# Splitting one granule's load over the DMA engines unevenly in a two-layer decode kernel

## The chip, the cores and the metric
The kernel runs on one core of a Trainium2 chip. The metric is the device time of one execution in microseconds. Sixteen DMA engines bring data from HBM to SBUF; the core's five compute engines are TensorE (PE), VectorE (DVE), ScalarE (ACT), GpSimd (POOL) and SyncE (SP), of which SP here only issues transfers.

## The reference
One decode step of two layers, each an attention block and a dense block, with the same weights and the same caches in both layers:

```python
B, Sq, D = 8, 1, 512
Hq, Hkv, Sk, Dh = 32, 8, 8192, 128
...
q = ((x @ wq).reshape(B, Sq, Hq, Dh)).transpose(0, 2, 1, 3)
scores = einsum("bhqd,bhkd->bhqk", q, repeat(k_cache, 4, axis=1)) * Dh ** -0.5
o = einsum("bhqk,bhkd->bhqd", softmax(scores), repeat(v_cache, 4, axis=1))
attention = o.transpose(0, 2, 1, 3).reshape(B, Sq, Hq * Dh) @ wo
dense = einsum("bsf,fd->bsd", silu(einsum("bsd,df->bsf", x, w1)), w2)
...
x = x + attention(layernorm(x));  x = x + dense(layernorm(x))     # twice
```

All inputs are bfloat16. K and V together hold 2 x 8 x 8 x 8192 x 128 elements, 268 MB, and every key and value is needed in both layers.

## The kernel before
**Granules and slots.** The 8192 keys of one head and batch are cut into four granules of 2048 keys. A granule of K or V is 512 KB: 128 partitions, on each 16 consecutive keys of 128 elements, which is one contiguous row of 4096 bytes in HBM and in SBUF. The SBUF tensor `ARENA` has 28 slots of this size. Some loads bring two neighbouring granules at once into two slots (`d.n == 2`, rows of 8192 bytes).

**Order.** A task is (layer, batch, head). `make_tasks` orders the 128 tasks so that the two layers of each batch interleave: heads 3 to 7 of a batch are kept heads, which are done for layer 0, then, once the batch's query for layer 1 is known, for layer 1. Of the kept heads' K granules (20, heads 3 to 7) the transposed keys stay in their slots from layer 0 to layer 1; of V only the last three granules stay (head 7, granules 1 to 3). One K granule (head 7, granule 3) is parked in PSUM in between. Thus K of head 7, granule 0 is read from HBM once for each batch, and V of it twice. The order of all loads comes from a planner (`lay_loads`), which gives each one a slot, a place in the order and a time from which the slot is free.

**Work on a granule.** Keys are transposed on PE (line 551) and copied back over the granule by ACT (line 560) and DVE (line 562); scores are matmuls on line 585; the softmax runs over the whole head (lines 596 to 634); the product with V is on line 645. The order of the keys inside a granule does not matter as long as K and V have the same. The dense blocks and projections run between the tasks (lines 760 and 732).

**Loads.** All big loads are issued on SP's queue by `issue` through the helper `dma` (line 407). `dma` waits (line 88, in `Sync.wait`) for what last used the slot, takes a token of the slot's own semaphore, which counts 16 for each transfer, and issues the transfer. A consumer waits until the semaphore has reached the token's value. `issue_until` issues loads in the planned order, and its place among the compute steps sets which readers a load waits for.

The program itself is a long unrolled list of instructions, which the chip fetches by DMA while it runs: these transfers appear in the profile as queues of the kind "instruction".

## Time and profile before

| What | Value |
|---|---|
| Median of 3 runs | 1132.41 us (1131.87 to 1133.05) |
| Profiled execution: time / span | 1138.0 us / 1136.2 us |
| PE, DVE, ACT busy | 82%, 49%, 43% of the span |
| Granted TensorE clock, mean | 0.933 |
| Read from HBM | 452.47 MB, 398 GB/s over the span |
| Loads of one granule (V / K) | 206 / 184, 512 KB each |
| Loads of two granules (V / K) | 141 / 84, 1024 KB each |

The profile is of one execution. A busy share says how long an engine had something to do, not that it was the limit. The queue lines give DMA packets (one for each contiguous row, and one of 4 bytes for each engine's addition to a semaphore), their bytes and the time that they took as a share of all 16 engines' span. A packet's record has its start, its length, its size and its queue, but not its engine.

### The profile page before, as it was taken

What the parts mean: (1) busy time and instruction counts of PE and PEld (TensorE: products, weight loads), DVE (VectorE), ACT (ScalarE), POOL (GpSimd) and SP (SyncE); (2) the same over time, 40 slices, a digit from 0 to 9 for tenths busy, and PEclk for the clock granted to TensorE, in tenths of its full rate; (3) what the DMA queues carried; (4) which work ended last, traced back from release to release, by engine and by line L of the source; (5) the groups of instructions that cost most, each with busy time, mean ns of one, the idle gap of its engine ahead of it and who ended that gap; (6) DMA issues with size and microseconds to landing.
All of it is one profiled execution on the core that took longest, in us unless ns stands there. A gap on an engine that the chain in (4) does not pass through costs nothing.

```text
span 1136.2 us, 42713 instructions
## 1 busy us (share of the span) xinstructions
PE 930.5 (82%) x18792; PEld 699.6 (62%) x18792; DVE 555.3 (49%) x1710; ACT 492.2 (43%) x778; POOL 117.8 (10%) x300
## 2 busy tenths in 40 slices
PE   6687888888888788888888888888888887878886
PEld 4366656666576556666566655666566665766565
DVE  6444554456344544446444554445444463445544
ACT  5354424554255424554245433554245442544332
POOL 0000110011100110001100111001100111001100
PEclk9699988999899988999699998999899997999987
DMA  9999999999999999999999999999999999999995
GB/s 377 416 414 414 393 406 419 417 396 404 416 418 412 334 400 419 417 409 383 399 419 412 387 399 420 418 412 397 407 418 414 398 401 413 418 413 376 400 418 221
DMA packets 91805, 455.25 MB, mean 401 GB/s; under 512 B 10204, under 2 KB 10468, under 8 KB 62308
## 3 DMA queue, kind: packets, MB, share of 16 engines
q1 hardware_dynamic: 91604, 452.51, 98.9%
q8 instruction: 148, 2.42, 0.9%
q14 instruction: 37, 0.30, 0.1%
q10 hardware_dynamic: 16, 0.01, 0.0%
HBM read 452.47 MB, written 0.01 MB: 398 GB/s over the span
## 4 chain that ended last, share of the span: by engine, by line
DMA 49%; PE 33%; DVE 8%; ACT 4%; issue 4%; SPq 2%; POOL 0%; POOLq 0%; ACTq 0%; DVEq 0%
DMA arena<-in_A_v_cache_dram 29%; DMA arena<-in_A_k_cache_dram 18%; PE TPp L551 15%; PE SCp L585 8%; DVE arena L562 7%; PE OTp L645 4%; ACT arena L560 3%; PE MISC L760 3%; DMA wq<-in_A_wq_dram 2%; PE TPp L625 2%; SPq L407 2%; ACT P L609 1%; PE KEPTp L551 1%; DVE small L634 0%; PE MISC L732 0%
## 5 line engine op out<-in xcount | busy, mean ns | idle before, releaser
L560 ACT COPY arena<-TPp 128x1024 bf16<-128x1024 bf16 x344 | 348.3, 1013 | 388.8 <-PE TPp L551 385.6
L562 DVE COPY arena<-TPp 128x1024 bf16<-128x1024 bf16 x344 | 238.0, 692 | 335.7 <-PE TPp L551 333.7
L551 PE MATMUL TPp<-ident,arena 128*128 128x128 bf16 x5504 | 378.8, 223 | 25.9 <-DMA arena<-in_A_k_cache_dram 19.5
L551 PEld LDWEIGHTS TPp<-ident,arena 128*128 128x128 bf16 x5504 | 318.4, 100 | 112.5 <-issue 64.2
L645 PE MATMUL OTp<-PT,arena 128*128 128x32 bf16 x8192 | 291.3, 179 | 59.4 <-DMA arena<-in_A_v_cache_dram 54.1
L645 PEld LDWEIGHTS OTp<-PT,arena 128*128 128x128 bf16 x8192 | 251.9, 97 | 133.7 <-DMA arena<-in_A_v_cache_dram 100.7
L585 PE MATMUL SCp<-arena,QB 128*32 128x512 bf16 x2048 | 221.5, 421 | 73.0 <-DVE arena L562 27.2
L609 ACT ACTIVATE P<-SCp,small 128x512 bf16<-128x512 f32 x128 | 88.0, 688 | 205.6 <-DVE small L607 169.3
L596 DVE TENSOR_REDUCE small<-SCp 128x1 f32<-128x512 f32 x128 | 88.4, 691 | 96.2 <-PE SCp L585 95.0
L585 PEld LDWEIGHTS SCp<-arena,QB 128*32 128x32 bf16 x2048 | 60.3, 95 | 115.5 <-ACT arena L560 52.1
L600 POOL PARTITION_ALL_REDUCE small<-small x128 | 47.7, 373 | 576.9 <-DVE small L598 576.9
L617 POOL PARTITION_ALL_REDUCE small<-small x128 | 55.4, 433 | 327.4 <-DVE at L659 147.9
L625 PE MATMUL TPp<-ident,P 128*128 128x128 bf16 x512 | 55.0, 235 | 30.4 <-ACT arena L560 17.4
L625 PEld LDWEIGHTS TPp<-ident,P 128*128 128x128 bf16 x512 | 31.4, 103 | 40.1 <-ACT arena L560 24.1
L629 DVE COPY PT<-TPp 128x256 bf16<-128x256 bf16 x128 | 37.3, 291 | 21.6 <-PE TPp L625 19.9
L615 DVE TENSOR_SCALAR small<-small 128x4 f32<-128x4 f32 x128 | 28.7, 224 | 31.1 <-ACT P L609 30.8
L598 DVE TENSOR_SCALAR small<-small 128x4 f32<-128x4 f32 x128 | 29.4, 230 | 4.5
L773 DVE STREAM_TRANSPOSE MISC<-MISC 128x128 f32<-128x128 f32 (+2 forms) x40 | 22.0, 550 | 18.0 <-PE MISC L760 18.0
L605 DVE TENSOR_TENSOR small<-small 128x4 f32<-128x4 f32 x128 | 20.0, 156 | 20.9 <-POOL small L600 20.9
L609 ACT ACTIVATION_READ_ACCUMULATOR P<-SCp,small 128x1 f32 x128 | 24.7, 193 | 0.0
L760 PE MATMUL MISC<-wo,at 128*32 128x128 bf16 x1024 | 24.6, 221 | 0.0
L560 ACT COPY arena<-KEPTp 128x1024 bf16<-128x1024 bf16 x16 | 16.2, 1012 | 14.3 <-PE KEPTp L551 10.9
(102 smaller groups left out, 331.6 us busy)
## 6 DMA issues: line engine op xcount, KB each, us to landing
arena<-in_A_v_cache_dram SPq DMA_DIRECT2D x141, 1024.0 KB, 19.6
arena<-in_A_v_cache_dram SPq DMA_DIRECT2D x206, 512.0 KB, 7.0
arena<-in_A_k_cache_dram SPq DMA_DIRECT2D x184, 512.0 KB, 9.4
arena<-in_A_k_cache_dram SPq DMA_DIRECT2D x84, 1024.0 KB, 22.0
arena<-in_A_wo_dram SPq DMA_DIRECT2D x8, 512.0 KB, 12.7
wq<-in_A_wq_dram SPq DMA_DIRECT2D x1, 4096.0 KB, 25.3
w<-in_B_w_dram SPq DMA_DIRECT2D x1, 1792.0 KB, 23.3
arena<-in_B_w_dram SPq DMA_DIRECT2D x3, 512.0 KB, 17.3
```

What stands on the lines that cost most here:

```text
L551: lambda c=c: pe.transpose(tpv[:, c, :], chunk(slot, h * GRP + c), ident[:, :])
L560: op(act, lambda: act.copy(dst, bank[:, :]), reads=[rt], writes=[r_half(slot, h)])
L562: op(dve, lambda: dve.tensor_copy(dst, bank[:, :]), reads=[rt], writes=[r_half(slot, h)])
L585: lambda t=t: pe.matmul(SCp[bank][t * QR:(t + 1) * QR, :], QB[qn][:, NGRAN - 1 - k:NGRAN - 1 - k + QR], keys[:, t * KB:(t + 1) * KB], star ...
L596: op(dve, lambda: dve.tensor_reduce(mxp[st][:, :], SCp[bank][:, :], AX.X, ALU.max), reads=[f"SC{bank}"], writes=[f"mxp{st}"])
L600: op(pool, lambda: pool.partition_all_reduce(mxa[st][:, :], mxr[st][:, :], 128, bass.bass_isa.ReduceOp.max), reads=[f"mxr{st}"], writes=[f ...
L609: op(act, lambda: act.activation(P[:, :], SCp[bank][:, :], ACT.Exp, bias=nb[st][:, 0:1], scale=SM_SCALE, accum_out=rs[st][:, :]), reads=[f ...
L617: op(pool, lambda: pool.partition_all_reduce(ssa[st][:, :], ssm[st][:, :], 128, bass.bass_isa.ReduceOp.add), reads=[f"ssm{st}"], writes=[f ...
L625: lambda c=c: pe.transpose(tpv[:, c, :], P[:, c * 128:(c + 1) * 128], ident[:, :])
L629: op(dve, lambda: dve.tensor_copy(PT[:, :, :, :], tpv.rearrange("p c (t q) -> p c t q", q=QR)[:, :, :, 0:NGRAN * REP]), reads=[f"TP{tb}"], ...
L645: lambda n=n, cc=cc: pe.matmul(otp, chunk(slot, n), PT[:, cc % CPB, (cc // CPB) % NT, cc // (CPB * NT)::NGRAN].unsqueeze(2).to_broadcast([ ...
L760: lambda t=t, col=col, w=w, start=start, stop=stop: pe.matmul(MISC[t * QR:(t + 1) * QR, 0:math.prod(w.shape[1:])], spread(col), w, start=s ...
```

## The change
The load of granule 0 of head 7, of K and of V, becomes two transfers into the same slot. The first fills partitions 0 to 47 with the granule's rows 0 to 47 in another order: partition 8a + p gets row 6p + a, and the source's access pattern has the six values of a as its outermost dimension. The second fills partitions 48 to 127 with rows 48 to 127 as usual. Both add to the slot's semaphore, and consumers wait for both. All other loads stay one transfer; `dma` takes a list of parts for this.

```diff
+FEW = 6
+SHARE = 8
+UNEVEN = (7, 0)
...
-    def dma(eng, out_ap, in_ap, counter, reads=(), writes=()):
+    def dma(eng, parts, counter, reads=(), writes=()):
...
         syn.acquire(eng, reads, writes)
-        tok = counter.next_tok()
-        eng.dma_start(out_ap, in_ap).then_inc(counter.sem, 16)
+        for out_ap, in_ap in parts:
+            tok = counter.next_tok()
+            eng.dma_start(out_ap, in_ap).then_inc(counter.sem, 16)
         syn.release(tok, reads, writes)
         return tok
...
         dst = ARENA[:, d.slot * SLOT:(d.slot + d.n) * SLOT]
-        dma(sp, dst, src, slsem[d.slot],
+        parts = [(dst, src)]
+        if (d.g, d.k) == UNEVEN:
+            assert d.n == 1
+            m = FEW * SHARE
+            parts = [(dst[0:m], src[0:m].rearrange("(p a) e -> a p e", a=FEW)), (dst[m:128], src[m:128])]
+        dma(sp, parts, slsem[d.slot],
             writes=[r_half(s, h) for s in range(d.slot, d.slot + d.n) for h in range(HALVES)])
```

The other calls of `dma` only put their one pair into a list.

More of the change, by code (lines that the diff above doesn't have):

```diff
@@ L441, in _ @@
         def _(sync_eng):
-            dma(act, Xr[0:B, :], x_in, wsem["x"], writes=["P"])
+            dma(act, [(Xr[0:B, :], x_in)], wsem["x"], writes=["P"])
             op(pool, lambda: pool.memset(ident[:, :], 0.0), writes=["ident"])
@@ L480, in load_wq @@
             def load_wq():
-                dma(sp, wq_sb[:, :, :], A_wq.rearrange("(kt p) n -> p kt n", p=128), wsem["wq"], writes=["wq"])
+                dma(sp, [(wq_sb[:, :, :], A_wq.rearrange("(kt p) n -> p kt n", p=128))], wsem["wq"], writes=["wq"])
             def load_rest():
-                dma(sp, w1_sb[:, :, :], B_w1.rearrange("(kt p) f -> p kt f", p=128), wsem["w1"], writes=["w1"])
-                dma(sp, w2_sb[:, FT - FT % RUN:, :], B_w2[(FT - FT % RUN) * 128:, :].rearrange("(ft p) d -> p ft d", p=128),
+                dma(sp, [(w1_sb[:, :, :], B_w1.rearrange("(kt p) f -> p kt f", p=128))], wsem["w1"], writes=["w1"])
+                dma(sp, [(w2_sb[:, FT - FT % RUN:, :], B_w2[(FT - FT % RUN) * 128:, :].rearrange("(ft p) d -> p ft d", p=128))],
                     wsem["w2"], writes=["w2"])
@@ L492, in load_runs @@
                 for (w, _to, _name, g), s in zip(runs, lent):
-                    dma(sp, ARENA[:, s * SLOT:(s + 1) * SLOT],
-                        w[g * RUN * 128:(g + 1) * RUN * 128, :].rearrange("(p i) d -> p (i d)", i=RUN), slsem[s],
+                    dma(sp, [(ARENA[:, s * SLOT:(s + 1) * SLOT],
+                              w[g * RUN * 128:(g + 1) * RUN * 128, :].rearrange("(p i) d -> p (i d)", i=RUN))], slsem[s],
                         writes=[r_half(s, h) for h in range(HALVES)])
```

## The prediction
> **What bounds the kernel now.** I read the busy table by slices first, then the DMA queues, the chain that ended last, the DMA issues, and the waits of SP's queue.

> ```profile
> DMA  9999999999999999999999999999999999999995
> GB/s 377 416 414 414 393 406 419 417 396 404 416 418 412 334 400 419 417 409 383 399 419 412 387 399 420 418 412 397 407 418 414 398 401 413 418 413 376 400 418 221
> DMA packets 91805, 455.25 MB, mean 401 GB/s; under 512 B 10204, under 2 KB 10468, under 8 KB 62308
> ## 3 DMA queue, kind: packets, MB, share of 16 engines
> q1 hardware_dynamic: 91604, 452.51, 98.9%
> q8 instruction: 148, 2.42, 0.9%
> q14 instruction: 37, 0.30, 0.1%
> ...
> DMA 49%; PE 33%; DVE 8%; ACT 4%; issue 4%; SPq 2%; POOL 0%; POOLq 0%; ACTq 0%; DVEq 0%
> ```

> The DMA row is full in 39 of 40 slices, and the transfers hold the largest part of the chain. The one line that matters for this change is q8: 148 packets that are no data but instruction fetches. 37,584 of the 42,713 instructions are PE's matmuls and weight loads, so nearly all of q8 is PE's program.

> ```profile
> SPq L88 <- PE OTp L645: 426.1, 232, 6.8
> SPq L88 <- PE SCp L585: 138.2, 142, 6.9
> ```

> ```profile
> L407 SPq DMA_DIRECT2D arena<-in_A_v_cache_dram x347: 327/328/4997, 14.8 to 1102.8; - x174
> ```

> The queue that issues the loads waits over 560 us for PE to release slots (first two lines, from the waits of SP's queue: total, times, longest), and an issue itself takes 0.33 us (the line from the view of source line 407: shortest, median, longest in ns). So SP has time to spare; slots and the 16 DMA engines set the pace.

> A share of 0.9% hides that fetches need not be spread evenly, so I went through the trace's packets one by one. A 4096-byte row of a granule takes 159 ns and the next row of the same engine starts 3 or 4 ns before its end: 155.5 ns a row. By this and by the count of eight rows and one mark (4 bytes, for the semaphore) per engine and granule, each engine's packets can be followed from the start to about 120 us. Three things come out.
> - A q8 fetch (16,384 bytes, mean 1.05 us) sits on one engine and sets that engine back by 1.54 to 1.61 us, in 11 clear cases of the first 120 us: ten rows, far more than its bytes. The others lose nothing.
> - The first eight fetches fell on eight different engines; the ninth and tenth on the two that had the first two (they were equally late, so their order can't be told). So I read a rotation over eight of 16. The small q14 fetches (8,192 bytes; 0.68 to 0.98 us lost) fell on others, as far as it can be told.
> - The spread from first to last of the 16 landings of one granule averages 2.9 us and reaches 5.3 us, with some six engines close together in front. It grows over the stretches of each batch where the queue is ten deep, and is drained where it is four deep.

> So the eight fetch engines are the bound: 148 / 8 = 18.5 fetches x 1.56 us = 28.9 us over the run in which the rest must wait, 3.6 us in each batch's cycle of about 140 us. That agrees with the spread.

> **The change, part by part.** K of granule (7,0) is read once a batch (kept for layer 1), V twice: 8 x 3 = 24 granules; the order of all other instructions and of the 629 loads on SP stays.

> *Which engines.* Before, each of 16 engines has 8 rows. The first new transfer has six as outermost dimension, and the trace shows what that does: the output store, whose outermost dimension is 4, has 5 updates of its semaphore where a granule has 16 (one for each of 4 engines, one from the queue for the rest), and the load of x with 8 rows has 9. So 48 rows go to six engines, 8 each, and the 80 rows to sixteen, 5 each. Six engines get 13 rows, ten get 5.

> *Rows.* Six engines: 24 x 5 = 120 rows more, x 155.5 ns = +18.7 us. Ten: 24 x 3 = 72 fewer, -11.2 us. A further mark for each of the six: 24 x 6 ns = 0.1 us. Bytes stay the same.

> *Issues.* 24 more on SP, 0.33 us each, 7.9 us. They hide behind SP's wait of over 560 us; the next load behind one comes 0.33 us later. If that cover were gone, all 7.9 us would count. I take 0.

> *Landing.* A split granule is complete when the longest engine is: 5 x 155.5 = 0.78 us later where the six were no earlier than the rest, and nothing where they lead by 3 to 5 us. What would be late next is PE's line 645 or 551, both of which already wait for such loads.

> *Sum, if the six are not fetch engines.* Eight fetch engines: 28.9 - 11.2 = 17.7 us. The six: 18.8 us, and their part of the small fetches: 37 x 0.8 us = 30 us, over the eight other engines 3.7 us each: 22.5 us. The largest falls from 28.9 to 22.5: -6.4 us. If the small fetches missed the six entirely it would be -10.1 us; if two or three engines of the six held all of them, 18.8 + 10 to 15 us: 0 to +5 us. The small ones that could be placed fell on different engines, so I take the even share. Not all of it can reach the end: the last 11 us move no loads, and a third of the chain is PE's, so that in places a load is early enough already. As an estimate I take five sixths, -5.4 us.

> *Unknown: the pace of the rows.* [...] From below: 155.5 ns, as the loads of wo, of w and of both caches have it, with different row orders; from above: 331 to 441 ns, as a row beside a fetch. At twice the pace the 8 rows would cost the six 24 x 8 x 155.5 = 30 us more. The many rows at 155.5 ns are nearer, and I take that. A gain from the pace itself is excluded: no full-size row in the trace is faster.

> [...]

> **Rivals.**
> 1. *The six include fetch engines: slower.* No row names engines. If even one of the six is among the eight, it has 28.9 + 18.7 = 47.6 us and the kernel gets up to 18.7 us longer: 1151 us. It decides from one shared engine on. For it: eight of 16 are fetch engines; six blindly chosen would miss them rarely. Against it: the load of x ran on eight engines, and five of them can be told, since a first row starts exactly 6 ns after x's mark. Following these five, one or two got a fetch and three or four none, so of the first eight fetches at most two fell on these five. I read it as two fetch engines among x's eight and six free ones. If x's load takes the same end of the row of engines as the new transfer, with the two at its far end, the six are clear.
>    [...]
> 2. *No difference.* The lead of the six may be used up by the small fetches, or PE (82% busy, 33% of the chain) takes over as soon as loads come earlier. For it: SP waits for PE, not for a transfer. Against it: PE's own waits for the caches' loads sum to 100.7 + 54.1 + 47.0 us. Time: 1130.2 to 1134.7.
> 3. *The rows are slower, or small fetches pile up on the six.* Then the six are the bound: +2 to +14 us, 1134.7 to 1146. It decides once the six lose 6.4 us more than reckoned, 0.27 us a split granule. Against it: row pace hardly varies.
> 4. *The change does not do what it says*, and all 16 engines share the 48 rows: 3 + 5 rows, no change. The store's 5 updates speak against it; it is counted with rival 2.

> **How the numbers follow.** The profiled execution took 1138.0 us (span 1136.2 and 1.8 around it), 5.6 us above the median of 1132.41; the difference is taken over as it is. Forecast: 1132.4 - 5.4 = 1127.0. A measurement tells about 0.2%, 2.3 us, from no change. Chances: faster as reckoned 0.62 (1121.5 to 1130, with -10.1 as lower end), no difference 0.11, rival 3 0.10, rival 1 0.17. With rival 1 left out, and the top of rival 3, the range is 1121.5 to 1144. The forecast's own range is 1121.5 to 1130.

> **What would show it.** The page should have 91,604 + 24 x 6 = 91,748 packets on q1, with q8 unchanged at 148. The mean spread of a granule's landings should shrink below 2.9 us, and the GB/s of the full slices should rise by half a percent. The sums of PE's waits for both caches (L645, L551) should fall. For a split granule's first transfer, 6 engine landings and one update from the queue would be seen. Wrong: the spread grows, with six landings last at every split granule (rival 1 or 3); rows of the 48 clearly above 159 ns (rival 3); spread smaller yet the same time (rival 2).

## The result, and the profile after

The changed kernel takes 1218.7 us (median of six runs, 1213.8 to 1227.4), the kernel before 1132.2 us beside it (six runs, 1129.6 to 1136.5). The ratio is 1.0766, with a 95% interval of 1.0724 to 1.0807: 86.7 us slower, where 5.4 us less was forecast. It lies far outside the range.

From the page of the changed kernel, the rows of the slices, the queues and the chain's engines:

```profile
DMA  9999999999999999999999999999999999999995
GB/s 379 416 416 340 372 414 382 375 318 386 388 419 331 372 400 392 388 366 383 385 402 345 317 412 380 417 340 344 401 385 375 338 389 378 418 366 319 402 385 233
DMA packets 91951, 455.25 MB, mean 374 GB/s; under 512 B 10349, under 2 KB 10613, under 8 KB 62453
q1 hardware_dynamic: 91748, 452.51, 98.5%
q8 instruction: 148, 2.42, 0.8%
...
DMA 58%; PE 27%; DVE 6%; SPq 3%; issue 3%; ACT 3%; POOL 0%; POOLq 0%; ACTq 0%; DVEq 0%
```

The program's transfers are what was reckoned: 91,748 packets on q1, which is 91,604 + 24 x 6, the same bytes, 148 fetches. The DMA row is as full as before. But the GB/s row, which had one dip below 370 inside the run, now dips to between 317 and 345 in nine slices of it. The engines are busy the whole time (98.5% on q1) and move less: single rows take longer, those of 4096 bytes 181.3 ns in the mean for 166.4. The chain agrees: transfers carry 58% of it, 49% before.

PE's waits for the caches' loads (total us, times, longest), before and then after:

```profile
PEld OTp L645 <- DMA arena<-in_A_v_cache_dram: 100.7, 169, 2.5
PE OTp L645 <- DMA arena<-in_A_v_cache_dram: 54.1, 120, 2.1
...
PEld TPp L551 <- DMA arena<-in_A_k_cache_dram: 47.0, 93, 2.6
...
PE TPp L551 <- DMA arena<-in_A_k_cache_dram: 19.5, 40, 2.3
```

```profile
PEld OTp L654 <- DMA arena<-in_A_v_cache_dram: 146.4, 181, 3.5
PE OTp L654 <- DMA arena<-in_A_v_cache_dram: 97.6, 132, 3.4
...
PEld TPp L560 <- DMA arena<-in_A_k_cache_dram: 75.4, 109, 3.6
PE TPp L560 <- DMA arena<-in_A_k_cache_dram: 40.9, 56, 3.3
```

The trace's packets give the size. Rows of 4096 bytes (51,328 of them) take 181.3 ns in the mean where they took 166.4, and one in twenty now takes over 293 ns (171 before); rows of 8192 bytes (29,312) take 329.9 ns, 315.8 before. Per engine that is 51,328 x 14.9 ns / 16 = 47.8 us and 29,312 x 14.1 ns / 16 = 25.8 us, together 73.6 us of the 80.4 by which the profiled span grew (1216.6 less 1136.2). None of the 8192-byte rows belongs to a split granule: at least 25.8 of the 73.6 us are lost by transfers that the change doesn't touch.

Where it happens is seen at the first split granule. It is issued at about 72 us, and its rows land between 95.9 and 101.2 us. The windows of before, and then of after (start:end, length, busy us of PE, PEld, DVE, ACT, POOL, granted clock, DMA share, GB/s):

```profile
90.00:95.00 5.00, 2.88 (x48) 2.23 (x45) 1.84 (x5) 1.79 (x3) 0.37 (x1) 0.85 1.00 412
95.00:100.00 5.00, 4.98 (x96) 4.03 (x94) 1.93 (x6) 2.02 (x2) 0.43 (x1) 0.81 1.02 410
100.00:105.00 5.00, 4.04 (x85) 3.44 (x83) 2.53 (x6) 3.18 (x6) 0.37 (x1) 1.00 1.02 416
```

```profile
90.00:95.00 5.00, 2.92 (x46) 2.28 (x44) 1.78 (x5) 1.79 (x3) 0.37 (x1) 0.73 1.02 401
95.00:100.00 5.00, 4.17 (x49) 3.27 (x47) 1.93 (x6) 2.02 (x2) 0.43 (x1) 0.59 1.03 253
100.00:105.00 5.00, 4.22 (x104) 3.61 (x104) 1.88 (x4) 1.82 (x3) 0.21 (x1) 1.00 1.00 394
```

In one stretch of 5 us the rate falls from 410 to 253 GB/s with a full DMA share (it is slightly above 1, as a row begins 3 to 4 ns before the one ahead of it ends), and PE does about half as many matmuls. The stretches beside it are nearly as before. What is missing is 157 GB/s x 5 us = 0.79 MB, 12 rows on each of 16 engines, or 1.9 us. Over all 24 splits the packets show the same. In the 7 to 15 us in which the rows of one split run, all rows together take 2.1 to 4.0 us more, in the mean of the sixteen engines, than at their usual 159 and 312 ns. That makes 74 of the 104 us by which the rows of the whole run exceed these lengths; before it was 31 us in all.

### The profile page after: what moved, and what is told of

Same layout as the page of the kernel before. It is cut to its first block, busy times and chain, and to the rows that moved or that the text cites. A ratio compares the mean times of both kernels' runs of the same rounds, so it can differ in the third digit from the quotient of the medians.

```text
span 1216.6 us, 42737 instructions
## 1 busy us (share of the span) xinstructions
PE 952.9 (78%) x18792; PEld 718.2 (59%) x18792; DVE 555.5 (46%) x1710; ACT 491.5 (40%) x778; POOL 117.3 (10%) x300
## 2 busy tenths in 40 slices
DMA  9999999999999999999999999999999999999995
DMA packets 91951, 455.25 MB, mean 374 GB/s; under 512 B 10349, under 2 KB 10613, under 8 KB 62453
## 3 DMA queue, kind: packets, MB, share of 16 engines
q1 hardware_dynamic: 91748, 452.51, 98.5%
q8 instruction: 148, 2.42, 0.8%
## 4 chain that ended last, share of the span: by engine, by line
DMA 58%; PE 27%; DVE 6%; SPq 3%; issue 3%; ACT 3%; POOL 0%; POOLq 0%; ACTq 0%; DVEq 0%
DMA arena<-in_A_v_cache_dram 40%; DMA arena<-in_A_k_cache_dram 15%; PE TPp L560 12%; PE SCp L594 6%; DVE arena L571 5%; PE OTp L654 5%; SPq L411 3%; PE MISC L769 2%; ACT arena L569 2%; DMA wq<-in_A_wq_dram 2%; PE TPp L634 2%; ACT P L618 1%; PE MISC L741 0%; DVE small L614 0%; DVE small L605 0%
## 5 line engine op out<-in xcount | busy, mean ns | idle before, releaser
L560 PE MATMUL TPp<-ident,arena 128*128 128x128 bf16 x5504 | 398.2, 230 | 47.2 <-DMA arena<-in_A_k_cache_dram 40.9
L560 PEld LDWEIGHTS TPp<-ident,arena 128*128 128x128 bf16 x5504 | 335.4, 103 | 139.8 <-DMA arena<-in_A_k_cache_dram 75.4
L594 PE MATMUL SCp<-arena,QB 128*32 128x512 bf16 x2048 | 225.0, 429 | 68.2 <-DVE arena L571 28.7
L643 DVE RECIPROCAL small<-small 128x4 f32<-128x4 f32 x128 | 21.7, 170 | 0.9
## 6 DMA issues: line engine op xcount, KB each, us to landing
arena<-in_A_v_cache_dram SPq DMA_DIRECT2D x141, 1024.0 KB, 18.7
```

Of the source, the lines that this page charges most:

```text
L560: lambda c=c: pe.transpose(tpv[:, c, :], chunk(slot, h * GRP + c), ident[:, :])
L594: lambda t=t: pe.matmul(SCp[bank][t * QR:(t + 1) * QR, :], QB[qn][:, NGRAN - 1 - k:NGRAN - 1 - k + QR], keys[:, t * KB:(t + 1) * KB], star ...
```

## The experiments

Every kernel is the changed one with other lines in place of the split; `m` is 48, `SLOT` the bf16 elements of one row (4096 bytes), `FEW` and `SHARE` are the constants 6 and 8. The kernel before ran beside each.

**Which part of the change costs it?** Four kernels move all the rows, in four ways.

```
e1  parts = [(dst[0:m], src[0:m]), (dst[m:128], src[m:128])]
e2  parts = [(dst, src.rearrange("(p a) e -> a p e", a=16))]
e3  ... src[0:m].rearrange("(p a) e -> a p e", a=16) ...   # FEW replaced
e4  parts = [(dst[0:64], src[0:64]), (dst[64:128], src[64:128])]
```

> The same 24 granules in the same two transfers of 48 and 80 partitions, but rows in their usual order, so that both transfers run on 16 engines (3 and 5 rows each) and no engine has more rows than before. Theory P (engines write partitions that in whole granules belong to other engines, and meet the other engines' traffic there): rows of all engines are slow around each split as in the changed kernel, +40 to +90 us. Theory S (the reordered source rows slow the reads): no slow rows, 0 to +5 us. Theory F (it takes the six engines and their 13 rows): 0 to +5 us.

Measured: 1202.73 us, ratio 1.0592 (1.052 to 1.0665), about +67 us.

> The 24 granules in one transfer of 128 partitions each, but with the source rows reordered (sixteen as outermost dimension, an engine's eight rows 64 KB apart), so 16 engines with 8 rows each. Theory S: slow rows, +40 us or more. Theory P: the partitions of a whole granule are dealt out as before only if the engines' shares are the same as in an ordinary load; then 0 to +3 us. Theory F: 0.

Measured: 1203.34 us, 1.0598 (1.0539 to 1.0657), +68 us.

> The changed kernel with sixteen in place of six as outermost dimension: 48 reordered rows over 16 engines, 3 each, then 80 rows, 5 each. Theory P: as e1, +40 to +90 us. Theory S: slower than e1 by what the order costs. Theory F (only the six engines' load matters): 0 to +5 us.

Measured: 1202.19 us, 1.0588 (1.0533 to 1.0642), +67 us.

> The 24 granules in two ordinary transfers of 64 partitions, 16 engines with 4 rows each. Theory P: an engine writes other partitions than in a whole granule unless whole granules are dealt out in the same halves, +20 to +90 us. Theories S and F: 0 to +5 us, for one more transfer and its marks.

Measured: 1205.07 us, 1.0613 (1.0514 to 1.0712), +69 us.

Four kernels, one price. e1 and e4 keep the order of the rows, so the order is not it (theory S). None has six as its outermost dimension (in the changed kernel such a transfer has 7 landings, six engines and the queue; the plain one of 80 rows has 16), so the six engines are not it (theory F), though six add something: after is 1.0766, some 20 us more than e3. e2 is a single transfer, so their number is not it. What is left is how a granule's rows are divided: between two groups of partitions in e1, e3 and e4, and by an outermost dimension of sixteen on the source's side in e2. The window of e4, without any reordered row, shows the same hole (e1, e2 and e3 have 253, 261 and 239 GB/s there):

```profile
90.00:95.00 5.00, 2.90 (x46) 2.25 (x44) 1.75 (x5) 1.79 (x3) 0.37 (x1) 0.74 1.01 397
95.00:100.00 5.00, 2.99 (x49) 2.41 (x47) 1.86 (x6) 2.02 (x2) 0.43 (x1) 0.91 1.02 258
```

The theory that fits is P of the expectations, by which a row gets in the way where it is written by another engine than in a usual load. No packet names its engine or its partition, so which rows those are in e1 to e4 is not shown, and P stays the author's reading of the four prices.

**Is it the division of the rows?** e5 also makes two transfers of a granule, but of all 128 partitions each. f1, f2 and f3 load only some partitions (the others of these 24 loads are left out), with eight (f1) or six (f2, f3) as outermost dimension and eight rows for each of its values over the two transfers; f3 is f2 on partitions 64 higher. The author assumed that in f1 and f2 every row stays with its usual engine, and that in f3 none does; no trace shows it.

```
e5  parts = [(dst[:, 0:SLOT // 2], src[:, 0:SLOT // 2]), (dst[:, SLOT // 2:SLOT], src[:, SLOT // 2:SLOT])]
f1  parts = [(dst[o:o + 32], src[o:o + 32].rearrange("(p a) e -> a p e", a=8)) for o in (0, 32)]
f2  parts = [(dst[o:o + 24], src[o:o + 24].rearrange("(p a) e -> a p e", a=6)) for o in (0, 32)]
f3  as f2, for o in (64, 96)
```

> The 24 granules in two transfers again, but cut along the row: 128 partitions each, 2048 bytes of every row, so that each transfer is dealt out over the engines like an ordinary one. Theory P (engines meet on each other's partitions): no slow rows beyond the shorter packets, 0 to +6 us. Theory T (any second transfer, semaphore count or issue makes the rows slow): +40 to +70 us as in the 48 + 80 and 64 + 64 splits.

Measured: 1132.35 us against 1132.54, 1.0015 (0.9979 to 1.0052): nothing.

> Of the 24 granules only partitions 0 to 63 are loaded (the upper half keeps what was in the slot), in two transfers of 32 partitions with eight as outermost dimension: eight engines with 8 rows as in a whole granule, eight with none. [...] The eight engines without rows save 192 rows x 155.5 ns = 29.9 us. If the fetch engines are all among them, the time falls by up to 25 us; if two fetch engines are among the eight that keep their rows, these stay the bound and the time changes by less than 8 us. Theory R (any shape but a whole granule is slow): +30 us or more.

Measured: 1131.86 us, 0.9984 (0.9947 to 1.002).

> [...] Theory P: no slow rows. If the six are free of fetches, the fetch engines save 29.9 us and the time falls by 15 to 28 us, clearly more than with eight engines if two of those eight are fetch engines. Theory R: +30 us or more.

Measured: 1130.56 us, 0.9969 (0.9946 to 0.9992).

> [...] Theory P: rows slow around each of the 24, the time 20 to 70 us above f2_six_own. If the partitions written don't matter: as f2_six_own within 5 us.

Measured: 1181.07 us, 1.0425 (1.0341 to 1.051), +48 us.

f3 less f2 is 50 us for 48 rows per split. The landings of every load are as many in both, and q1 has 89,588 packets and 444.64 MB in both: 91,604 less 24 x 144, and 48 transfers of 24 rows and six marks, so both use six engines. Below, the window of the split and PE's waits in f2, and then in f3:

```profile
95.00:100.00 5.00, 4.86 (x97) 4.03 (x96) 1.87 (x6) 2.03 (x3) 0.43 (x1) 0.84 1.01 410
```

```profile
95.00:100.00 5.00, 2.43 (x50) 1.76 (x47) 1.96 (x6) 1.64 (x2) 0.43 (x1) 1.00 1.00 288
```

```profile
PEld OTp L653 <- DMA arena<-in_A_v_cache_dram: 90.5, 146, 2.0
PE OTp L653 <- DMA arena<-in_A_v_cache_dram: 49.7, 101, 1.7
```

```profile
PEld OTp L653 <- DMA arena<-in_A_v_cache_dram: 124.4, 182, 2.5
PE OTp L653 <- DMA arena<-in_A_v_cache_dram: 76.5, 137, 2.3
```

Only where the rows are written differs in f3, and, since a granule's rows follow its partitions, which rows of the cache are read. The hole and the longer waits come with it. Of the rows that start between 94 and 101 us in f3, one in ten takes over 320 ns (4096 bytes) or over 613 ns (8192 bytes), twice the usual 159 and 312; in f2 nine in ten take at most 165 and 319 ns. In e5's window, two transfers of 128 partitions each, there is none:

```profile
95.00:100.00 5.00, 4.86 (x91) 3.82 (x89) 1.93 (x6) 1.55 (x2) 0.43 (x1) 0.73 1.02 404
```

So it is shown that the place of the rows, where they are written or, with it, where they are read, costs this: two transfers that are free on partitions 0 to 23 and 32 to 55 cost 2.1 us a granule on 64 to 87 and 96 to 119. Splitting along the row (e5), two issues (e5, f1, f2) and eight or six as outermost dimension (f1, f2) do not. That the difference is who usually writes there, as P has it, is not shown: it fits the rows at twice their length, but no row of a trace names an engine. The read side was changed by itself only between e1 and e3, where the first 48 rows come in another order at the same price; that f3 reads other rows than f2 is not ruled out by a run of its own.

**Does it go by the number of splits?** e11 is e4 with only K split, 8 granules of 24.

```
if d.kind == "K":
    parts = [(dst[0:64], src[0:64]), (dst[64:128], src[64:128])]
```

> The two ordinary transfers of 64 partitions for K alone, 8 granules in place of 24. Theory P (each such split costs by itself, where engines meet on partitions): a third of the cost of e4_plain_64_64, +18 to +27 us. If a few splits are enough to put the engines out of step for good: more than half, over +33 us.

Measured: 1155.25 us against 1132.91, 1.0199 (1.0168 to 1.023), +22.5 us; a third of e4's 69 us is 23. A granule loaded as 64 and 64 partitions costs 2.8 to 2.9 us, whether of K alone or of K and V.

**What are fewer rows worth?** f4 and f5 are like f2 with four and five as outermost dimension (32 and 40 rows of the 128; the rest is left out). f0 loads only the first 128 bytes of each row.

```
f4  parts = [(dst[o:o + 16], src[o:o + 16].rearrange("(p a) e -> a p e", a=4)) for o in (0, 32)]
f5  the same with 20 rows and a=5
f0  parts = [(dst[:, 0:64], src[:, 0:64])]
```

> Of the 24 granules only the first 128 bytes of each row are loaded, in one transfer of 128 partitions: all 16 engines save nearly all of 192 rows, 29.9 us. Theory B (the eight fetch engines' work is the bound): the time falls by 20 to 29 us. Theory C (PE and the release of slots are the bound, and the DMA engines only look full): it falls by less than 6 us.

Measured: 1125.24 us against 1132.91, 0.9938 (0.9914 to 0.9962), -7 us.

> [...] Theory C: as f0_narrow, less than 6 us.

Measured: 1123.05 us, 0.9924 (0.99 to 0.9949), -8.6 us.

> [...] Theory C: less than 6 us.

Measured: 1124.98 us, 0.9912 (0.9874 to 0.9949), -10 us.

This bears on the forecast's sum. In f0 a row takes 13 ns instead of 159, so all sixteen engines, whichever get the fetches, are relieved of 24 x 8 x 146 ns = 28 us, and the time falls by a quarter of that, far from the five sixths of the forecast and near theory C. The chain that ended last says where the rest went. In f0 it runs through PE more than through transfers, while before it was DMA 49% and PE 33%:

```profile
PE 43%; DMA 32%; DVE 13%; ACT 6%; issue 5%; SPq 1%; POOL 0%; POOLq 0%; ACTq 0%; DVEq 0%
```

Transfers and PE's own work are so close in this kernel that a relief of one soon leaves the other in front, although q1 is still busy for 98.2% of the span. f2 leaves ten engines without any of the eight rows and gains 3.5 us. f5 and f4 gain 8.6 and 10 us, more than theory C's 6 and less than the 15 that f2's expectation has for engines free of fetches. Whether the engines that keep their rows are free of them can't be read from differences this small against their intervals; it stays open.

**What do more rows on fewer engines cost?** Four kernels vary the changed one's six engines and eight rows. With fewer engines the longest engine's rows grow. The outermost dimension is taken for the number of engines, as it is in the changed kernel's first transfer (six, 7 landings), the output store (four, 5) and the load of x (eight, 9).

```
g12  FEW = 12, SHARE = 4
g8   FEW = 8,  SHARE = 6
g4   FEW = 4,  SHARE = 12
g3   FEW = 3,  SHARE = 16
```

> The 48 reordered rows on twelve engines (4 each, 9 with the second transfer). Both theories: 67 + 24 x 1 x 155.5 ns = +71 us.

Measured: 1194.62 us against 1129.32, 1.056 (1.0505 to 1.0614), +63 us.

> The 48 reordered rows on eight engines (6 each, 11 with the second transfer). Theory B, with two fetch engines among them: 67 + 24 x 3 x 155.5 ns = 67 + 11.2 = +78 us. Theory N: the same, +78 us.

Measured: 1210.39 us, 1.0702 (1.0648 to 1.0755), +79 us.

> The changed kernel with its 48 reordered rows on four engines (12 each, 17 with the second transfer). Theory B (meetings cost 67 us; extra rows count in full on a fetch engine, and on a free one only beyond the fetch engines' 28.9 us): 67 + (24 x 9 rows x 155.5 ns = 33.6, + 3.7 for small fetches, - 28.9) = +75 us. Theory N (rows on few engines count in full wherever they are): 67 + 33.6 = +101 us.

Measured: 1220.55 us, 1.0796 (1.0739 to 1.0853), +90 us.

> The 48 reordered rows on three engines (16 each, 21 with the second transfer). Theory B: 67 + (24 x 13 x 155.5 ns = 48.5, + 3.7, - 28.9) = +90 us. Theory N: 67 + 48.5 = +115 us.

Measured: 1249.08 us, 1.104 (1.0983 to 1.1098), +118 us.

With 80 rows on sixteen engines and 48 on some, the longest has SHARE - 3 rows above its usual eight, x 24 x 155.5 ns:

| engines for the 48 rows | extra rows of the longest | reckoned, us | measured, us |
|---|---|---|---|
| 16 (e3) | 0 | 0 | +67 |
| 12 | 1 | 3.7 | +63 |
| 8 | 3 | 11.2 | +79 |
| 6 (the change) | 5 | 18.7 | +87 |
| 4 | 9 | 33.6 | +90 |
| 3 | 13 | 48.5 | +118 |

Each price is uncertain by about 6 us. From sixteen engines to three it rises by 51 us for 48.5 reckoned. Over the row as a whole, extra rows are paid nearly in full, on top of the 67 us. The theory that a lead of free engines takes them up expected about 75 us for four and 90 for three, and fell. The steps between are uneven: twelve engines cost no more than sixteen, and four hardly more than six, 11 us below 67 + 33.6. Why these two steps are so small isn't settled.

No kernel that loads everything was faster than the one before; e5 equals it.

## Why the prediction was wrong, point by point

*The bound.* Partly right. When rows slow down, the time follows. The rotation of the fetches over eight engines fits f2 too: followed packet by packet, the ninth fetch seems to hit the engine of the first again (in f2 at 18.1 and 90.7 us), though no record names it. But that the eight hold the rest back by their full 28.9 us, so that a relief of them reaches the end, is not borne out: f0 relieved all engines by 28 us and saved 7, and PE took over the chain.

*What the change does.* Right: the packets, the fetches, and the six landings with one update from the queue at a split's first transfer. Rival 4 is out.

*Rows and issues.* The count was right as far as it went. Five extra rows on six engines were put at 18.7 us, and the change stands 20 us above e3, which has none. Issues at nothing: e5 has the same 24 more, and takes no longer.

*The pace of the rows.* This is the step that failed. "I take that", it says of 155.5 ns, since many loads with different row orders run at it; but all of those are loads of 128 partitions in one transfer, with these as the outermost dimension on both sides, and the order of rows was not what mattered: e1 and e3 differ in it and take 1202.7 and 1202.2 us. Its upper end charged twice the pace to the six engines' own eight rows (30 us). In fact the pace drops for the rows of neighbouring transfers too, by 73.6 us per engine in the mean over the run, so the bound was drawn around the wrong rows.

*Landing.* Said to cost 0.78 us or nothing. The mean spread of the landings of whole granules grew from 2.95 to 3.68 us instead of shrinking; its growth was half of the sign that the prediction gave for rivals 1 and 3.

*The sum.* Wrong even without that step. It credited the six with a lead that could be spent; the table above shows extra rows paid for nearly in full from sixteen engines to three. And the pass-through of five sixths is about a quarter in f0. Two slips are too small to matter: five sixths of 6.4 is 5.3, not 5.4, and 10.1 less gives 1122.3, not 1121.5.

*The rivals.* Rival 1 had the right side and, by the change's 20 us over e3, about the right price for its own part, but the closeness of 20 to 18.7 does not speak for its reason, a shared fetch engine, which no run shows. Rival 3 had the right kind, slower rows, with a ceiling of 14 us. Neither contained 87.

## What to carry to other kernels

Where the DMA queues are as full as here (q1 98.9%), split a load along the row, over all 128 partitions (e5: 0 us), not between partitions (e1, e4: 2.8 to 2.9 us for each of these granules), and keep the 128 partitions as the outermost dimension on both sides (e2: 2.8 us). A full DMA row says that engines are occupied, not that they move bytes at their pace (a share of 1.03 at 253 GB/s in the changed kernel's window, 1.02 at 410 before); read it beside the GB/s row, and compare a window around the edit before and after. When an edit divides the rows of a load in another way, look at the rows of the loads around it too, and bound an unknown pace over all the engines that could be disturbed, not over the edited rows alone: here at least 25.8 of 73.6 us were lost by rows that the edit does not touch.
